# Query and key stages of a polysketch attention kernel: 32x32 TensorE tiles for the large units, and outer products with one factor in PSUM

## Chip, core and metric

The kernel runs on one core of a Trainium2 chip. The metric is the time on the device, in microseconds, of one execution. TensorE is called PE here, VectorE DVE, ScalarE ACT, GpSimd POOL and SyncE SP, as in the profile.

## What is computed

Four batches of four heads have q, k and v of 1088 positions by 32, and two sketches S1 and S2 of 8 x 32. The attention replaces the softmax by a product of two sketches; its result, with the heads side by side, goes through a two-layer network with the activation elu.

```python
def phi(x):
    a = np.einsum('rd,bhsd->bhsr', S1, x)
    b = np.einsum('rd,bhsd->bhsr', S2, x)
    return np.einsum('bhsi,bhsj->bhsij', a, b).reshape(*x.shape[:-1], r * r)
q_p, k_p = (phi(q), phi(k))
kv = np.einsum('bhsf,bhsd->bhfd', k_p, v)
z = np.sum(k_p, axis=2)
num = np.einsum('bhsf,bhfd->bhsd', q_p, kv)
den = np.einsum('bhsf,bhf->bhs', q_p, z)[..., None] + 1e-06
...
h = x @ w_in                              # 4352 x 128 by 128 x 2048
g = np.where(h > 0.0, h, alpha * (np.exp(np.minimum(h, 0.0)) - 1.0))
return (g @ w_out).astype(np.float32)     # 2048 x 128
```

Everything is float32. A feature vector is the outer product of two vectors of 8, so 64 numbers for each position and head.

## The kernel before, in words

**Steps.** The 68 half tiles of 64 positions (17 in each batch) are taken in nine groups g of eight, the last of four. d_ff is cut into eight pairs cp of 128 columns. A step is one (g, cp); the loop at L944 writes them out in a fixed order: groups 0 and 1 in turn, then groups 2 to 8, each with its eight cp. In step n PE computes `mm1` of step n (two PSUM tiles `h`, four buffers, L226), ACT and DVE make elu of it (`e`, two activations at L748 and L750; `gg`, L756), and PE then does the second matmul of step n-2. For groups 2 to 7 this second matmul is `mm2_seven` (L674): seven products of half size in place of eight, whose sums of the moving operand POOL makes (`tt`, L667 to L672). `W` holds the weights.

**The attention between the steps.** A table (`at`, `mid`, `late`, from L862) hangs single functions on a step: `at(n)` after mm1 of step n, `mid(n)` after the first half of elu, `late(n)` after the second half. Within an engine the order is the order of the calls; it is written out by hand and no scheduler changes it. Waits between engines follow from the tiles and their buffers.

- *Keys of batches 1 to 3* (L898): `transp` transposes k; `KF_late` (L315) projects it with 64x32 tiles of PE into two PSUM banks, `kfps`; `KF_late_out` transposes these to `abk` on DVE; `KO` (L334) forms the outer product `kp`, in two halves of 1280 and 1024 elements, on POOL for batch 1 and on DVE for batches 2 and 3; `KA` (L366) multiplies with v into the bank `kv`; `turn` and `turned` give `kvq` (L403, with a mask that keeps every second head) and the part of the denominator that is added to `SWq` (L395).
- *Queries of groups 2 to 8*, in units (L485): a unit is one group, or from group 4 on two groups. `un` counts its half tiles for each half of the partitions: 4 for units 2 and 3, 8 for units 4 and 6, 2 for unit 8. `queries` (L622) runs at steps 13, 15, 22, 30, 46 and 62, each time with q5 of one unit and q1 of the next: q5 with f = 0, then q1, then q5 with f = 1. `q1` (L502) multiplies the transposed q with `SWq`, `q1_out` transposes the result on DVE to `abw`; `q2_den` (L525) and `q2_half` (L580) form the quotient `an` and the outer product `qp` on DVE, `q4` transposes it to `qpT`; `q5` (L595) multiplies with `kvq`, and `q5_out` copies the result on ACT to `xg`, the input of mm1.

**Tiles of PE.** q1 and q5 use the array as four 64x64 tiles. A unit's positions are cut into two runs w, and the heads into two pairs r; in q1 the pair of heads is the row half and the run the column half, in q5 the other way round. A row half has a PSUM bank of its own. With 64 rows and two heads, the masked weights (`cmask`, the zeros of `SWq`) make half of the products zero. A matmul's length is the number of half tiles of its run that lie in one batch (`parts`, L492).

**PSUM.** Eight banks: four `h`, one each of `o0` and `o1`, and two with the tag `aux`, which the kfps, kv and query results share in turn. Where the results of q5 and q1 don't fit side by side in the two aux banks, `queries` takes the two `h` banks of the next step as well, before mm1 of that step writes them.

**Outer products.** `q2_half` and `KO` multiply a factor that is repeated along the inner axis by one that is repeated along the middle axis:

```python
nc.vector.tensor_mul(qp[g, i][:, :m], _ap(a_, list(a_.ap[1:]) + [[0, R]]),
                     _ap(b_, [b_.ap[1], [0, R], b_.ap[2]]))
```

Both factors lie in SBUF here.

Of the kernel before, what the change touches and what calls it, by code (L numbers as in the profile page):

```python
# [12 lines left out]
F32 = mybir.dt.float32  # L13
# [9 lines left out]
def _ap(ap: bass.AP, free):  # L23
    return dataclasses.replace(ap, ap=[list(ap.ap[0])] + [list(x) for x in free])
# [3 lines left out]
def kernel(  # L28
# [21 lines left out]
    nc = tc.nc  # L50
    B, H, S, D = q.shape
    R = S1.shape[0]
    P = 128
    FD = H * D
# [4 lines left out]
    KT = (NT + 1) // 2  # L59
# [4 lines left out]
    const = ctx.enter_context(tc.tile_pool(name="const", bufs=1))  # L64
    work = ctx.enter_context(tc.tile_pool(name="wk", bufs=2))
    psum = ctx.enter_context(tc.tile_pool(name="psum", bufs=2, space=bass.MemoryType.PSUM))
# [6 lines left out]
    qT = [const.tile([FD, NT, 64], F32, name=f"qT{b}") for b in range(2)] * 2  # L73
# [142 lines left out]
    cmask = const.tile([P, 2], F32, name="cmask")  # L216
# [12 lines left out]
    def keep_warm(n, cols=256):  # L229
        for i in range(n):  # L230
            nc.tensor.matmul(idle[:, :cols], some[:, :P], some[:, :cols], skip_group_check=True)  # L231
# [26 lines left out]
    Sab = const.tile([FD, H, 2 * R], F32, name="Sab")  # L258
    SW = const.tile([FD, H, 3, R], F32, name="SW")
    SWq = const.tile([FD, B, 2, 4, R], F32, name="SWq")  # L260
    keep_warm(3)
    keep_warm(1, 128)
    sps = psum.tile([P, 512], F32, name="sps", tag="aux")
# [24 lines left out]


    kvS = const.tile([P, H, D], F32, name="kvS")  # L290
    kvq = const.tile([P, B, 2, H, D], F32, name="kvq")
    kv_ps, kvz, feats, wzs, kf_ps = {}, {}, {}, {}, []


# [32 lines left out]
    def KF_late_out(b):  # L327
        ps = feats[b]
        ab = feats[b] = work.tile([P, 2, KT, H, R], F32, name="abk", tag="abk", bufs=2)
        for g2 in range(2):  # L330
            nc.vector.transpose(ab[:, :, :, 2 * g2:2 * g2 + 2, :].rearrange("p x t c r -> p t x (c r)"),
                                ps[g2][:, :32 * KT].rearrange("p (t x y) -> p t x y", x=2, y=2 * R))

    def KO(b, half, eng=nc.vector):  # L334
        kp = work.tile([P, 5, H, R, R], F32, name="kp", tag="kp", bufs=3)
# [59 lines left out]
    def Z_share(b):  # L395
        z = wzs.pop(b)
        nc.gpsimd.tensor_add(SWq[:, b, :, 2, :], z[:, :2], z[:, 2:])

    def KV(b, ps):
        for f in range(2):  # L400
            halves(ps[:, 128 + P * f:128 + P * f + P], kvz[b][:, f].rearrange("p c s -> p (c s)"), ident[:])

    def KV_out(b, ps):  # L403
        nc.vector.tensor_mul(kvq[:, b].rearrange("p f (g c) d -> p (f g) c d", c=2),
                             ps[:, 128:384].rearrange("p (x c d) -> p x c d", c=2, d=D),
                             _ap(cmask[:], [[0, 4], [1, 2], [0, D]]))


    def Z_first():
# [21 lines left out]
    NQ = (NH + 7) // 8  # L431
    qn = [min(8, NH - 8 * g) // 2 for g in range(NQ)]
    abw, ans, qp, qpT, xg, xps = {}, {}, {}, {}, {}, {}
# [4 lines left out]
    def half_tile(g, k):  # L438
        return divmod(8 * g + k, NT)
# [45 lines left out]
    units = {g: ([g, g + 1] if 4 <= g < NQ - 1 else [g]) for g in [2, 3] + list(range(4, NQ, 2))}  # L485
    un = {g: sum(qn[x] for x in gr) for g, gr in units.items()}
# [2 lines left out]

    def parts(g, w):  # L492

        n = un[g]
        k = 0
        while k < n:
            b, t = half_tile(g, n * w + k)
            m = min(n - k, NT - t)
            yield b, t, k, m
            k += m  # L500

    def q1(g, ps, start, o):  # L502
        todo = [(j, w, r, x) for w in range(2) for r in range(2) for j, x in enumerate(parts(g, w))]
        for j, w, r, (b, t, k, m) in sorted(todo, key=lambda x: x[0]):
            rows = slice(64 * r, 64 * r + 64)
            nc.tensor.matmul(ps[r][64 * w:64 * w + 64, o + 64 * k:o + 64 * (k + m)],  # L506
                             SWq[rows, b].rearrange("p c x r -> p (c x r)"),
                             qT[b][rows, t:t + m, :].rearrange("p t s -> p (t s)"), start=start and j == 0, stop=True,
                             skip_group_check=True, tile_position=(64 * r, 64 * w))
        abw[g] = ps, o  # L510

    def q1_out(g):
        (ps, o), n = abw[g], un[g]
        pair = n > 4
        abw[g] = work.tile([P, H * n if pair else H * 4, 4 * R], F32, name="abw", tag="abwp" if pair else "abw",
                           bufs=1 if pair else 2)
        for r in range(2):
            nc.vector.transpose(abw[g][:, 2 * n * r:2 * n * r + 2 * n, :].rearrange("p m y -> p (m y)"),
                                ps[r][:, o:o + 64 * n])

    def q2(g, parts=1):
        q2_den(g)
# [54 lines left out]
    def heads(g):  # L577
        return 2 if un[g] > 4 else H

    def q2_half(g, i):  # L580
        m = heads(g) * un[g]
        r = slice(m * i, m * i + m)
        qp[g, i] = work.tile([P, 4 * H, R, R], F32, name="qp", tag="qp", bufs=2)
        a_, b_ = ans[g][:, r], abw[g][:, r, :R]
        nc.vector.tensor_mul(qp[g, i][:, :m], _ap(a_, list(a_.ap[1:]) + [[0, R]]),
                             _ap(b_, [b_.ap[1], [0, R], b_.ap[2]]))

# [5 lines left out]
                            qp.pop((g, i))[:, :m].rearrange("p m i j -> p (m i j)"))  # L593

    def q5(g, ps, f):  # L595
        n = un[g]
        todo = [(j, w, r, x) for r in range(2) for w in range(2) for j, x in enumerate(parts(g, w))]
        for j, w, r, (b, t, k, m) in sorted(todo, key=lambda x: x[0]):
            i, o = (r, 0) if n > 4 else (0, 2 * n * r)
            rows = slice(64 * w, 64 * w + 64)  # L600
            nc.tensor.matmul(ps[w][64 * r:64 * r + 64, 64 * k:64 * (k + m)],  # L601
                             kvq[rows, b, f, 2 * r:2 * r + 2, :].rearrange("p c d -> p (c d)"),
                             qpT[g, i][rows, o + 2 * k:o + 2 * (k + m), f, :],
                             start=(f == 0 and j == 0), stop=(f == 1),
                             skip_group_check=True, tile_position=(64 * w, 64 * r))
        xps[g] = ps

    def q5_out(g, i=0):

        ps, n = xps[g], 64 * un[g]  # L610
        pair = len(units[g]) > 1
        x = xg[g + i] = work.tile([P, 512], F32, name="xg", tag="xg", bufs=3)
        for w in [i] if pair else range(2):
            if pair:
                to = x[:]
            elif g < NQ - 1:
                to = x[:, n * w:n * w + n]
            else:
                to = x[:, :2 * n].rearrange("p (k w s) -> p w k s", w=2, s=64)[:, w]
            nc.scalar.copy(to, ps[w][:, :n] if g < NQ - 1 else ps[w][:, :n].rearrange("p (k s) -> p k s", s=64))  # L620

    def queries(g5, g1, n):  # L622

        nx, nq = (64 * un[g] if g is not None else 0 for g in (g5, g1))
        if nx + nq > 512:
            hs[steps[n]] = [psum.tile([P, 512], F32, name="h", tag="h", bufs=4) for c in range(2)]
        aux = [psum.tile([P, 512], F32, name="qps", tag="aux") for _ in range(2)]
        if nx + nq > 512:
            xb, qb, o = [hs[steps[n]][0], aux[0]], [hs[steps[n]][1], aux[1]], 0
        else:  # L630
            xb, qb, o = aux, aux, nx

        if g5 is not None:
            q5(g5, xb, 0)
        if g1 is not None:
            q1(g1, qb, o == 0, o)
        if g5 is not None:
            q5(g5, xb, 1)


    hs, es, gs, ops = {}, {}, {}, {}
# [214 lines left out]
    steps = [(0, 0), (0, 1), (1, 0), (1, 1)] + [(g, cp) for cp in range(2, NP) for g in range(2)]  # L856
# [5 lines left out]
    def at(n, f, *a):  # L862
        extra.setdefault(n, []).append((f, *a))
# [4 lines left out]
    def late(n, f, *a):  # L868
        extra.setdefault((n, 1), []).append((f, *a))
# [22 lines left out]
    def turned(b):  # L892
        Z_out(b, kv_ps[b])
        KV_out(b, kv_ps[b])
        Z_share(b)


    for b, (n_t, n_f, n_o, n_a, n_z) in enumerate(  # L898
            ((4, 6, (7, 9), 11, 12), (15, 16, (17, 18), 19, 20), (17, 18, (23, 24), 27, 28)), 1):
        at(n_t, transp, kT, "k", b, 0, NT)  # L900
        at(n_f, KF_late, b)
        late(n_f, KF_late_out, b)
        for half in range(2):
            at(n_o[half], KO, b, half, nc.gpsimd if b == 1 else nc.vector)
        at(n_a, KA, b)
        late(n_a, sums_out, b)
        at(n_z, turn, b)
        late(n_z, turned, b)
# [16 lines left out]
    late(19, q2_half, 3, 0)  # L925
    late(20, q4, 3)
    late(22, q2_den, 4)
    at(26, q2_half, 4, 0)
    late(26, q2_half, 4, 1)
    late(27, q4, 4, 0)  # L930
    late(28, q4, 4, 1)
    late(31, q2_den, 6)
    late(32, q2_half, 6, 0)
    late(36, q2_half, 6, 1)
    late(37, q4, 6, 0)
    late(38, q4, 6, 1)
# [7 lines left out]
    for n in range(2, N + 2):  # L944
        if n < N:
            g, cp = steps[n]
# [26 lines left out]
        g, cp = steps[n - 2]  # L973
# [39 lines left out]
```

## Time and profile before

| | |
|---|---|
| timed runs | 269.57 us (268.58 to 269.76, three runs) |
| profiled execution, span | 267.13 us |
| PE, DVE, ACT, POOL busy | 98%, 71%, 68%, 62% |
| granted PE clock | 0.998 |
| DMA, mean | 51 GB/s, 49 GB/s of it HBM |

The profile is of one execution. An engine's busy time is the time in which it has an instruction in flight; matmuls overlap, so PE's share alone does not tell whether it is at its peak. Each float32 matmul of the code appears as two records, each with a weight load (PEld). "64*64 64x512" stands for a tile of 64 rows by 64 columns of the array and 512 moving columns. In a timeline a line gives start, length, engine, line of the kernel, operation, tiles and count; a bracket at its end gives the idle time of the engine before it and what ended that.

### The profile page before, as it was taken

The page shows a single profiled execution, that of the slowest core. Times are in us where ns is not written, and L with a number is a line of the kernel's source. Part 1 is how long each engine was busy: PE and PEld are TensorE (multiplying, and loading weights), DVE is VectorE, ACT ScalarE, POOL GpSimd, SP SyncE. Part 2 cuts the span into 40 slices and gives each one's busy share as a digit, 9 for nine tenths or more (in the row PEclk, how much of TensorE's full clock was granted, in tenths as well). Part 3 has the DMA queues.
Part 4 walks back from the last instruction along what each step waited for, and adds up shares of the span by engine and source line. Part 5 has one row for each costly group of instructions (what it writes and reads, how often), then busy time and mean ns, then how long its engine had stood idle before and what let it go on. Part 6 is the DMA issues. An engine that isn't in the chain of part 4 may idle for free.

```text
span 267.1 us, 7343 instructions
## 1 busy us (share of the span) xinstructions
PE 260.9 (98%) x2947; PEld 154.5 (58%) x2947; DVE 189.2 (71%) x342; ACT 181.5 (68%) x341; POOL 165.1 (62%) x230
## 2 busy tenths in 40 slices
PE   8899999999999999999999999999999999999994
PEld 6753333343333675658566666666766666666884
DVE  6799999996959896997649767554346444673652
ACT  2389978676566475766567777777677777777782
POOL 4400008204317986699969999998598888898300
PEclk9999999999999999999999999999999999999999
DMA  6996960011002200001100110001001100010011
GB/s 191 344 351 200 273 193 4 0 40 48 0 0 42 42 4 0 2 2 19 26 2 0 21 22 2 0 14 21 10 4 19 22 4 1 14 19 12 2 32 30
DMA packets 26418, 13.58 MB, mean 51 GB/s; under 512 B 19217, under 2 KB 24593, under 8 KB 26385
## 3 DMA queue, kind: packets, MB, share of 16 engines
q1 hardware_dynamic: 25792, 12.66, 18.2%
q8 instruction: 23, 0.38, 0.6%
q10 hardware_dynamic: 592, 0.46, 0.5%
q14 instruction: 11, 0.08, 0.1%
HBM read 10.88 MB, written 2.23 MB: 49 GB/s over the span
## 4 chain that ended last, share of the span: by engine, by line
PE 92%; DVE 4%; POOL 1%; ACT 1%; issue 1%; DVEq 0%
PE h L226 41%; PE pb L687 15%; PE pa L687 12%; PE o L226 11%; PE ol L226 3%; PE idle L231 2%; PE kv L371 1%; PE qps L601 1%; PE h L601 1%; DVE qp L549 1%; PE kfps L321 1%; PE h L506 1%; POOL tt L670 1%; PE kv L226 1%; PE abp L302 1%
## 5 line engine op out<-in xcount | busy, mean ns | idle before, releaser
L756 DVE SCALAR_TENSOR_TENSOR gg<-e,h 128x512 f32<-128x512 f32 (+1 forms) x144 | 92.4, 653 | 66.4 <-ACT e L750 65.1
L226 PE MATMUL h<-xg,W 128*64 128x512 f32 (+1 forms) x584 | 128.7, 563 | 0.0
L748 ACT ACTIVATE e<-h 128x512 f32<-128x512 f32 (+1 forms) x144 | 81.4, 565 | 56.1 <-PE h L226 52.9
L750 ACT ACTIVATE e<-e 128x512 f32<-128x512 f32 (+1 forms) x144 | 87.5, 607 | 4.4
L226 PEld LDWEIGHTS h<-xg,W 128*64 128x64 f32 x584 | 40.2, 137 | 47.3 <-issue 37.6
L670 POOL TENSOR_TENSOR tt<-gg 128x256 f32<-128x256 f32 x48 | 39.2, 817 | 12.1 <-DVE gg L756 11.6
L667 POOL TENSOR_TENSOR tt<-gg 128x256 f32<-128x256 f32 x48 | 35.1, 731 | 14.5 <-DVE gg L756 14.2
L672 POOL TENSOR_TENSOR tt<-gg,tt 128x256 f32<-128x256 f32 x48 | 38.4, 801 | 3.8
L671 POOL TENSOR_TENSOR tt<-tt,gg 128x256 f32<-128x256 f32 x48 | 36.0, 750 | 3.8
L687 PEld LDWEIGHTS pa<-gg,W 128*64 128x64 f32 x384 | 23.6, 137 | 23.7 <-issue 23.3
L226 PE MATMUL o<-gg,W 128*64 128x512 f32 x128 | 30.5, 597 | 0.4 <-DVE W L129 0.4
L687 PE MATMUL pa<-gg,W 128*64 128x128 f32 x384 | 29.5, 274 | 0.0
L687 PE MATMUL pb<-tt,SS 128*64 128x128 f32 x384 | 29.2, 273 | 0.0
L687 PEld LDWEIGHTS pb<-tt,SS 128*64 128x64 f32 x384 | 22.6, 137 | 0.0
L126 POOL TENSOR_TENSOR raw<-raw,tiny 128x512 f32<-128x512 f32 x1 | 1.0, 1045 | 29.8 <-DVE raw L121 29.8
L687 PE MATMUL pa<-tt,SS 128*64 128x128 f32 x192 | 18.7, 273 | 0.2 <-POOL tt L671 0.2
L687 PE MATMUL pb<-gg,SS 128*64 128x128 f32 x192 | 18.7, 273 | 0.0
L687 PE MATMUL pb<-tt,W 128*64 128x128 f32 x192 | 18.7, 273 | 0.0
L226 PEld LDWEIGHTS o<-gg,W 128*64 128x64 f32 x128 | 8.5, 136 | 16.2 <-issue 13.8
L687 PEld LDWEIGHTS pa<-tt,SS 128*64 128x64 f32 x192 | 12.1, 137 | 0.4 <-POOL tt L671 0.4
L687 PEld LDWEIGHTS pb<-gg,SS 128*64 128x64 f32 x192 | 12.1, 137 | 0.2 <-issue 0.2
L687 PEld LDWEIGHTS pb<-tt,W 128*64 128x64 f32 x192 | 12.2, 137 | 0.0
(139 smaller groups left out, 246.6 us busy)
## 6 DMA issues: line engine op xcount, KB each, us to landing
raw<-in_moe_w_in_dram SPq DMA_DIRECT2D x8, 256.0 KB, 5.5
raw<-in_moe_w_out_dram SPq DMA_DIRECT2D x8, 256.0 KB, 5.7
hd_k<-in_k_dram SPq DMA_DIRECT2D x3, 544.0 KB, 8.0
hd_q<-in_q_dram SPq DMA_DIRECT2D x3, 544.0 KB, 3.7
v<-in_v_dram SPq DMA_DIRECT2D x4, 288.0 KB, 6.8
out_dram<-ob SPq DMA_DIRECT2D x72, 16.0 KB, 1.5
v<-in_v_dram SPq DMA_DIRECT2D x4, 256.0 KB, 8.1
out_dram<-ob SPq DMA_DIRECT2D x16, 32.0 KB, 1.7
```

The source lines that it names most:

```text
L226: nc.tensor.matmul(dst[64 * u:64 * u + 64], lhs[:, 64 * u:64 * u + 64], rhs, skip_group_check=True, tile_position=(0, 64 * u), **kw)
L231: nc.tensor.matmul(idle[:, :cols], some[:, :P], some[:, :cols], skip_group_check=True)
L302: nc.tensor.matmul(ps[i // 5][64 * u:64 * u + 64, 64 * (i % 5):64 * (i % 5) + 64], kT[b][:, u * KT + i, :], Sab[:].rearrange("p h y -> p ( ...
L601: nc.tensor.matmul(ps[w][64 * r:64 * r + 64, 64 * k:64 * (k + m)], kvq[rows, b, f, 2 * r:2 * r + 2, :].rearrange("p c d -> p (c d)"), qpT[ ...
L667: nc.gpsimd.tensor_tensor(t[:, 0], b12, b11, op=SUB)
L670: nc.gpsimd.tensor_tensor(t[:, 2], b22, b12, op=SUB)
L671: nc.gpsimd.tensor_tensor(t[:, 1], t[:, 2], b11, op=ADD)
L672: nc.gpsimd.tensor_tensor(t[:, 3], b21, t[:, 1], op=SUB)
L687: nc.tensor.matmul(bank[64 * u:64 * u + 64, P * col:P * col + P], lhs, rhs[:, u], start=(first and i in (0, 3)), stop=last, skip_group_che ...
L748: nc.scalar.activation(e, hs[g, cp][c][:, :n], RELU, scale=-1.0)
L750: nc.scalar.activation(e, e, EXP, scale=-1.0)
L756: nc.vector.scalar_tensor_tensor(gs[g, cp][:, c, :n], es[g, cp][:, c, :n], -1.0, hs[g, cp][c][:, :n], op0=ADD, op1=MAX)
```

## The change

Units with `un` = 8 use sixteen 32x32 tiles, one head to a row or column quarter and four runs of positions, with the weights `SWs` (the sum of the two masked parts of `SWq`) and `kvs` (the unmasked kv). The other units keep 64x64. With four row quarters, q1 and q5 of these units write four banks (two `h` and two `aux`), 256 columns each. Where q5 and q1 of a call use different tiles, q5 with f = 0 and f = 1 now come one after the other, and q1 after both. `KO` of batches 2 and 3 and `q2_half` of units 4 and 6 read the factor `a` from an aux bank, to which ACT copies it a half step or more earlier. `KF_late` of batch 3 and its output move from step 18 to step 21, the first `q2_half` of unit 6 from step 32 to 33.

```diff
-    kvq = const.tile([P, B, 2, H, D], F32, name="kvq")
+    kvq = {b: const.tile([P, 2, H, D], F32, name=f"kvq{b}") for b in (0, 1, 3)}
+    kvs = {b: const.tile([P, 2, H, D], F32, name=f"kvs{b}") for b in (1, 2, 3)}
...
+    def KO_a(b, half):
...
+        p = feats[b, half, "a"] = psum.tile([P, 512], F32, name="ka", tag="aux")
+        nc.scalar.copy(p[:, :n], feats[b][:, 1, t].rearrange("p t h r -> p (t h r)"))
+    def KO_b(b, half):
...
+        nc.vector.tensor_mul(kp[:, :t.stop - t.start].rearrange("p t h i j -> p (t h) i j"),
+                             _ap(a_, list(a_.ap[1:]) + [[0, R]]), _ap(b_, [b_.ap[1], [0, R], b_.ap[2]]))
...
     def Z_share(b):
         z = wzs.pop(b)
         nc.gpsimd.tensor_add(SWq[:, b, :, 2, :], z[:, :2], z[:, 2:])
+        if b:
+            nc.gpsimd.tensor_add(SWs[:, b - 1], SWq[:, b, 0], SWq[:, b, 1])
...
     def KV_out(b, ps):
+        if b in kvs:
+            copy = nc.scalar.copy if b in kvq else nc.vector.tensor_copy
+            copy(kvs[b][:].rearrange("p f h d -> p (f h d)"), ps[:, 128:384])
+        if b in kvq:
...
+    def wide_tiles(g):
+        return un[g] < 8
     def parts(g, w):
-        n = un[g]
+        n = un[g] if wide_tiles(g) else un[g] // 2
...
+    def q1(g, ps, o, opened):
+        s = 64 if wide_tiles(g) else 32
+        n = P // s
+        todo = [(j, w, r, x) for w in range(n) for r in range(n) for j, x in enumerate(parts(g, w))]
...
+            nc.tensor.matmul(ps[r][s * w:s * w + s, o + 64 * k:o + 64 * (k + m)], lhs,
+                             qT[b][rows, t:t + m, :].rearrange("p t s -> p (t s)"),
+                             start=j == 0 and not any(ps[r] is x for x in opened), stop=True,
+                             skip_group_check=True, tile_position=(s * r, s * w))
...
     def q1_out(g):
-        for r in range(2):
+        m = H * n // len(ps)
+        for r in range(len(ps)):
...
+    def q2_a(g, i):
+        m = heads(g) * un[g]
+        p = psum.tile([P, 512], F32, name="qa", tag="aux")
+        ans[g, i] = p[:, :m * R].rearrange("p (m r) -> p m r", r=R)
+        nc.scalar.copy(p[:, :m * R], ans[g][:, m * i:m * i + m].rearrange("p m r -> p (m r)"))
...
     def queries(g5, g1, n):
+        banks = lambda g: 0 if g is None else 2 if wide_tiles(g) else 4
+        if banks(g5) + banks(g1) > 4:
             hs[steps[n]] = [psum.tile([P, 512], F32, name="h", tag="h", bufs=4) for c in range(2)]
         aux = [psum.tile([P, 512], F32, name="qps", tag="aux") for _ in range(2)]
+        ps = {2: aux, 4: hs.get(steps[n], []) + aux}
+        same = banks(g5) == banks(g1)
         if g5 is not None:
-            q5(g5, xb, 0)
+            q5(g5, ps[banks(g5)], 0)
+            if not same:
+                q5(g5, ps[banks(g5)], 1)
         if g1 is not None:
-            q1(g1, qb, o == 0, o)
-        if g5 is not None:
-            q5(g5, xb, 1)
+            q1(g1, ps[banks(g1)], 256 if g5 is not None else 0, ps[banks(g5)] if g5 is not None else [])
+        if g5 is not None and same:
+            q5(g5, ps[banks(g5)], 1)
...
-            ((4, 6, (7, 9), 11, 12), (15, 16, (17, 18), 19, 20), (17, 18, (23, 24), 27, 28)), 1):
+            ((4, 6, (7, 9), 11, 12), (15, 16, (17, 18), 19, 20), (17, 21, (23, 24), 27, 28)), 1):
...
-            at(n_o[half], KO, b, half, nc.gpsimd if b == 1 else nc.vector)
+            if b == 1:
+                at(n_o[half], KO, b, half, nc.gpsimd)
+            else:
+                late(n_o[half] - 1, KO_a, b, half)
+                at(n_o[half], KO_b, b, half)
...
+    for n, g, i in ((25, 4, 0), (26, 4, 1), (32, 6, 0), (35, 6, 1)):
+        late(n, q2_a, g, i)
...
-    late(32, q2_half, 6, 0)
+    late(33, q2_half, 6, 0)
```

q5 changes as q1 does, and `q5_out` copies two banks of 256 columns to each `xg` in place of one of 512.

## Prediction

> **What bounds the kernel now.** I read the page first, its busy shares and its chain of waits, then the timeline of single engines. A step is one pass of the loop at L944; I number steps by counting the groups of `h` matmuls.
>
> ```profile
> PE 260.9 (98%) x2947; PEld 154.5 (58%) x2947; DVE 189.2 (71%) x342; ACT 181.5 (68%) x341; POOL 165.1 (62%) x230
> ...
> PE 92%; DVE 4%; POOL 1%; ACT 1%; issue 1%; DVEq 0%
> PE h L226 41%; PE pb L687 15%; PE pa L687 12%; PE o L226 11%; PE ol L226 3%; PE idle L231 2%; PE kv L371 1%; PE qps L601 1%; PE h L601 1%; DVE qp L549 1%; PE kfps L321 1%; PE h L506 1%; POOL tt L670 1%; PE kv L226 1%; PE abp L302 1%
> ```
>
> TensorE is busy 98% and carries 92% of the chain. A busy PE need not be at its peak, so the starts in its timeline decide. Around step 30 (columns: start, length, engine, line, operation):
>
> ```profile
> 130.27 1.89 PE L226 MATMUL h<-xg,W 128*64 128x512 f32 x8
> 132.09 0.32 PE L601 MATMUL h<-qpT,kvq 64*64 64x128 f32 x1
> 132.09 0.64 PE L601 MATMUL qps<-qpT,kvq 64*64 64x512 f32 x1
> ...
> 133.01 0.59 PE L506 MATMUL h<-qT,SWq 64*64 64x512 f32 x1
> ...
> 133.87 0.59 PE L601 MATMUL qps<-qpT,kvq 64*64 64x512 f32 x1
> ...
> 134.83 0.66 PE L687 MATMUL pa<-gg,W 128*64 128x128 f32 x8
> ...
> 136.41 1.89 PE L226 MATMUL h<-xg,W 128*64 128x512 f32 x8
> 138.12 0.61 PE L687 MATMUL pa<-gg,W 128*64 128x128 f32 x8
> ...
> 139.65 1.89 PE L226 MATMUL h<-xg,W 128*64 128x512 f32 x8
> ```
>
> From 136.41 to 139.65 an ordinary step takes 3.24 us: 1.71 for eight `h` records, the rest for 28 records of L687. A pair of 512-column records on two column tiles takes 1.71/4 = 0.43 us, a pair of 128-column records 0.11: PE is bound by its columns, with no gap. So a column less on PE is time off the end, as long as nobody else makes PE wait.
>
> The query group of step 30 runs from 132.09 to 134.83. It has three phases, q5 f=0, q1 and q5 f=1, starting at 132.09, 133.00 and 133.87: 0.86 to 0.91 each, two 512-column records on each of four 64x64 tiles. It starts 0.10 after 130.27 + 1.72, and about 0.05 is lost in the first round after each change of tile size.
>
> Only one later stretch has PE waiting for another engine, steps 25 to 27:
>
> ```profile
> 111.07 1.37 DVE L286 TENSOR_TENSOR kp<-abk 128x1024 f32<-128x1024 f32 x1
> 111.32 1.72 POOL L670 TENSOR_TENSOR tt<-gg 128x256 f32<-128x256 f32 x1
> 113.11 0.73 POOL L671 TENSOR_TENSOR tt<-tt,gg 128x256 f32<-128x256 f32 x1
> ...
> 113.90 0.44 PE L687 MATMUL pa<-tt,SS 128*64 128x128 f32 x4 [0.16 <-POOL tt L671]
> ```
>
> POOL's L670, 0.73 elsewhere, takes 1.72 while DVE forms an outer product; `tt` is late, and PE with it. The L687 group at 113.13 lasts 1.91, the one at 116.76 lasts 1.71, where an undisturbed one lasts 1.53: 0.38 + 0.18, and 0.03 at 118.46, 0.59 us in all. DVE has no idle time from 105.92 to 123.
>
> **What the Trainium skill says.** "TensorE: Matmul & The Clock Gate", section "Measured speedup vs the span model": sixteen 32x32 tiles of 512 columns ran 10.6 times as fast as one after another, with about 4 ns between tiles. No run here has 32-row tiles; eight 64x32 tiles (`kfps`, 16 records of 288 columns) take 0.65 us from 85.64 to 86.29, where column time alone is 0.48, so eight do run side by side here. "TensorEngine Tiling (Array Packing)", "Key Properties": a change of tile size drains the array; the trace has 0.10 + 0.05 for it. "SBUF — State Buffer", "Who interferes with whom": a DVE operation with two SBUF inputs shuts out a GpSimd operation that reads SBUF, one with a single SBUF input does not; the 1.72 above agrees. "PSUM — Partial Sum Buffer", "PSUM bank collisions raise a hardware error": different row tiles may not write one bank at a time; the trace has one bank for each of the two row halves, and the change takes four for four.
>
> **The change part by part.** Sums are against the profiled span, 267.13 us; the three timed runs have a median of 269.57, and I carry the difference over.
>
> *32x32 tiles.* Only the two units with un = 8 change: 4 (q1 at step 22, q5 at 30) and 6 (q1 at 30, q5 at 46). Each tile streams 256 columns in place of 512, so a phase falls from 0.854 (4 x 0.427 / 2) to 0.427. Step 22: one phase, -0.43. Step 30: three, -1.28. Step 46: two, -0.85. Sum -2.56. Against it: steps 22 and 46 now mix both sizes, one change more each, 2 x 0.15 = +0.30. The tiles start one after another, some 7 ns apart (132.09 to 132.11 for four), so sixteen end about 0.08 later than four, in three groups: +0.25. The 40 records of a phase need 40 x 7 = 0.28 us to issue, under 0.427. **Net -2.0.** No 32-row tile is in the trace: if records cost 15 ns, as in the `kv` group (90 in 1.34), a phase takes 0.60 and six phases give back 1.0; if neither the extra change nor the stagger shows, -2.56. I take -2.0.
>
> *PSUM factor.* Eight outer products (KO for b = 2, 3, `q2_half` for units 4, 6) read one factor from PSUM. DVE: a 1024-element one takes 1.23 from PSUM (L354), the same as an undisturbed one from SBUF (69.41), but 1.34 to 1.70 while POOL works; 1280 elements 1.69 and 2.02, and about 1.23 + 256 x 1.04 ns = 1.49 from PSUM (the slope of L354: 256 elements 0.43, 1024 elements 1.23). In steps 23 to 27 DVE saves 0.53 + 0.14 + 2 x 0.12 = 0.9 and POOL three locks of about 0.95 (111.32, 118.30, and 120.91 at 1.60). PE's 0.59 goes: **-0.59**, with 0 as the other end. ACT gets eight copies: by L384 (32 elements, 0.17) and L620 (256, 0.38), about 0.9 ns an element, 0.26 to 0.29 each. ACT has 0.83 to 1.03 us idle before its first activation in nearly every step there; that hides them.
>
> *Waits added.* KO_a(b,0) stands in ACT's queue behind the two activations of its step and waits for DVE's KF_late_out (b = 2) or for q1_out to free the bank (b = 3); the next step's activations queue behind it. Then DVE waits for ACT before KO_b, with `gg` behind it, and PE wants `gg` two steps later. At 79.6 ACT has 1.83 us idle; at 105 it waited 0.72 anyhow. I take 0.
>
> *KF_late(3) from step 18 to 21.* Its PE time, 0.65 + 0.15, only moves: PE is 0.8 ahead from 18 to 21 and no more after. It passes KA(2), the turn of b = 2 and the groups of mm2. Its two DVE transposes (0.84) move from 88.84 to 100.77, where DVE has 1.30 us idle before 102.07. New is that q5(3) at step 22 needs the banks that they free: done near 101.0 to 101.6, against PE at 101.46. I take 0, at most 0.2.
>
> *q5 of one unit before q1 of the next (steps 22, 46).* ACT's two `xg` copies start at about 102.6 and not 103.47, so `gg` of step 22, 105.31 now, comes about 0.6 earlier, at the head of DVE's full stretch. q1_out takes four transposes of 0.39 for two of 0.70, +0.17 on DVE for each unit; q5_out four copies of 0.38 for two of 0.58, +0.35 on ACT: both beside PE, which is in L687 for 1.58 us after the group. At step 30 the two `h` banks are read first, some 0.9 us after PE leaves the group, before PE reaches the next `h`.
>
> *Small ones.* Three POOL adds of 0.22 (`SWs`): the first two stand in POOL's idle time (15.6 and 0.82), the third after `SWq` at 131.47, with q1(6) reading it 1.1 us or more later. `kvs`: two ACT copies of 0.37 with over 1.5 us idle before the next activation; b = 2 exchanges a DVE operation of 0.41 for a copy. All 0. No DMA is added, and SP's and POOL's queues keep their order.
>
> Sum: -2.0 - 0.59 = -2.6. Span 264.5, time 269.57 - 2.6 = **267.0 us**. About 0.5% (1.35 us) is what a measurement of this kernel tells from no change.
>
> **Rivals.**
> (a) *DVE keeps the stretch.* The locks go but the copies and the moved transposes keep DVE late; PE arrives earlier and waits the more, so that 0.6 to 1.4 of the 2.6 is lost: 267.6 to 268.4. For: no DVE idle from 105.92 to 123. Against: the 0.9 and 0.6 counted above.
> (b) *The tiles don't pay.* If only eight of sixteen stream at once, a phase stays at 0.854: +0.55 for changes and stagger, -0.59: 269.5, no change. For: no 32-row tile in the trace. Against: the 10.6 of the skill, `kfps`.
> (c) *Slower: the handshake.* Place: KO_b(3,0), KO_b(3,1), q2_half(4,0), q2_half(4,1) on DVE, steps 23 to 26. If each finds its ACT copy behind an activation pair (0.58 + 0.63 = 1.21), DVE loses 4 x 1.21 = 4.8, less the 1.2 that it gains net there, and PE, which now waits 0.59 and comes 0.3 earlier, waits 0.9 + 4.8 - 1.2 = 4.5 in all. -2.0 + (4.5 - 0.59) = +1.9: 271.5. It decides from some 4.3 us of DVE waiting. For: ACT and DVE now wait for each other in turn. Against: each copy is queued a step or half a step ahead, with ACT idle after it.
>
> **How the numbers follow.** Forecast 0.68 (266.0 to 267.6, the spread of -2.0 to -2.56 and of the runs); (a) 0.14, two thirds of it below 268.2; (b) 0.10; (c) 0.08. Faster 0.68 + 0.10 = 0.78; same 0.04 + 0.10 = 0.14; slower 0.08. The range 265.9 to 268.9 holds the forecast, (a) and the 15-ns records (268.0), and leaves (b) and (c) out.
>
> **What would show it.** Right: a query group of about 1.5 us at step 30; no L670 or L672 above 1.0 beside an outer product of b = 3 or of unit 4; L687 groups of 1.53 or 1.58 at steps 25 to 27; outer products of 1.23 and 1.49. Wrong: 32x32 records further apart than 15 ns; `ka` or `qa` copies that DVE waits for; PE waiting on an aux bank at step 22 or at KA(3) (step 27), whose bank q2_half(4,0) must free.

## The result and the profile after

| | before | after |
|---|---|---|
| timed runs, median | 269.16 us (268.58 to 269.76) | 267.84 us (267.27 to 268.26) |
| ratio, with 95% interval | | 0.9949 (0.9928 to 0.9971) |
| span of the profiled execution | 267.13 us | 266.5 us |
| first `kfps` matmul (step 4) to last matmul | 225.33 us | 224.24 us |
| query groups of steps 22, 30, 46 | 1.88, 2.74, 2.10 us | 1.82, 2.40, 1.97 us |
| `mm2_seven` groups of steps 25, 26 | 1.91, 1.71 us | 1.53, 1.53 us |

The change is faster by 1.3 us where 2.6 were forecast. The two spans differ by less still, because the start, up to the first `kfps` matmul, was 0.4 us longer in the profiled execution after; the fourth row leaves it out, and I use it for all kernels below: **1.09 us less**. A group's length is the time from its first matmul to the first of the next group. Line numbers of the kernel after: L542 is `q1`, L648 `q5`, L730 `mm2_seven`, L710 to L715 the sums `tt` on POOL, L350 `KO_b`, L628 `q2_half`.

The page of the kernel after, busy shares and chain:

```profile
PE 260.4 (98%) x3115; PEld 154.9 (58%) x3115; DVE 187.7 (70%) x346; ACT 183.9 (69%) x355; POOL 159.6 (60%) x233
...
PE 93%; DVE 4%; POOL 1%; issue 1%; ACT 0%; DVEq 0%
PE h L226 43%; PE pb L730 16%; PE pa L730 12%; PE o L226 11%; PE ol L226 3%; PE idle L231 2%; PE kv L391 1%; PE h L648 1%; PE qps L648 1%; DVE qp L586 1%; POOL kp L287 1%; PE kfps L323 1%; PE qps L542 1%; PE kv L226 1%; PE abp L304 1%
```

PE is the bound as before. It has 168 records more; POOL is busy 5.5 us less and `POOL tt` has left the chain. Step 30, PE's timeline (start, length, engine, line, operation, tiles, count of records):

```profile
131.89 0.41 PE L648 MATMUL h<-qpT,kvs 32*32 32x128 f32 x2
131.90 0.41 PE L648 MATMUL qps<-qpT,kvs 32*32 32x256 f32 x2
...
132.32 0.54 PE L648 MATMUL h<-qpT,kvs 32*32 32x128 f32 x5
132.58 0.36 PE L542 MATMUL h<-qT,SWs 32*32 32x192 f32 x2
...
133.29 0.40 PE L648 MATMUL h<-qpT,kvs 32*32 32x256 f32 x2
...
133.93 0.42 PE L648 MATMUL h<-qpT,kvs 32*32 32x128 f32 x5
134.29 0.66 PE L730 MATMUL pa<-gg,W 128*64 128x128 f32 x8
```

From 131.89 to 134.29 the three phases take 0.69, 0.59 and 1.12 (q5 f = 1 from 133.17), where 0.43 each was forecast. A phase is counted from its first matmul to the first of the next. The rows of 128 columns and five records are where the runs that a batch boundary cuts get their second matmuls.

The stretch where PE waited for POOL has gone. POOL's and PE's timelines at steps 25 and 26, with DVE's outer product at 110.96:

```profile
110.96 1.21 DVE L350 TENSOR_TENSOR kp<-ka,abk 128x1024 f32<-128x1024 f32 x1
```

```profile
111.21 0.73 POOL L713 TENSOR_TENSOR tt<-gg 128x256 f32<-128x256 f32 x1
112.02 0.73 POOL L714 TENSOR_TENSOR tt<-tt,gg 128x256 f32<-128x256 f32 x1
```

```profile
113.52 0.61 PE L730 MATMUL pa<-gg,W 128*64 128x128 f32 x8
113.95 0.39 PE L730 MATMUL pa<-tt,SS 128*64 128x128 f32 x4
```

The first `tt` beside the outer product takes 0.73, where it took 1.72, and no idle time stands behind the second matmul row of PE. Over the whole trace nine `tt` took more than 1 us before and two after; one of the two (1.60 at 93.91) lies beside the outer product of unit 3, which still reads both factors from SBUF.

So the sum has one good half and one bad: the waits gave back 0.59 as forecast, the tiles 0.53 in place of 2.0. The experiments ask first whether the halves stand alone, and then what the tiles pay.

### The profile page after: what moved, and what is told of

The parts are those of the page before. It is cut to its first block, busy times and chain, and to the rows that moved or that the text cites. A ratio compares the mean times of both kernels' runs of the same rounds, so it can differ in the third digit from the quotient of the medians.

```text
span 266.5 us, 7686 instructions
## 1 busy us (share of the span) xinstructions
PE 260.4 (98%) x3115; PEld 154.9 (58%) x3115; DVE 187.7 (70%) x346; ACT 183.9 (69%) x355; POOL 159.6 (60%) x233
## 4 chain that ended last, share of the span: by engine, by line
PE 93%; DVE 4%; POOL 1%; issue 1%; ACT 0%; DVEq 0%
PE h L226 43%; PE pb L730 16%; PE pa L730 12%; PE o L226 11%; PE ol L226 3%; PE idle L231 2%; PE kv L391 1%; PE h L648 1%; PE qps L648 1%; DVE qp L586 1%; POOL kp L287 1%; PE kfps L323 1%; PE qps L542 1%; PE kv L226 1%; PE abp L304 1%
## 5 line engine op out<-in xcount | busy, mean ns | idle before, releaser
L710 POOL TENSOR_TENSOR tt<-gg 128x256 f32<-128x256 f32 x48 | 35.1, 730 | 16.4 <-DVE gg L799 16.0
L713 POOL TENSOR_TENSOR tt<-gg 128x256 f32<-128x256 f32 x48 | 35.3, 736 | 14.4 <-DVE gg L799 14.0
L715 POOL TENSOR_TENSOR tt<-gg,tt 128x256 f32<-128x256 f32 x48 | 36.5, 760 | 3.8
L714 POOL TENSOR_TENSOR tt<-tt,gg 128x256 f32<-128x256 f32 x48 | 35.2, 733 | 3.8
L730 PEld LDWEIGHTS pa<-gg,W 128*64 128x64 f32 x384 | 23.6, 137 | 22.7 <-issue 22.0
L730 PE MATMUL pa<-gg,W 128*64 128x128 f32 x384 | 29.5, 275 | 0.0
L730 PE MATMUL pb<-tt,SS 128*64 128x128 f32 x384 | 29.1, 273 | 0.0
L730 PEld LDWEIGHTS pb<-tt,SS 128*64 128x64 f32 x384 | 22.6, 137 | 0.0
L730 PE MATMUL pb<-gg,SS 128*64 128x128 f32 x192 | 18.7, 273 | 0.0
L730 PE MATMUL pa<-tt,SS 128*64 128x128 f32 x192 | 18.6, 273 | 0.0
L730 PE MATMUL pb<-tt,W 128*64 128x128 f32 x192 | 18.6, 273 | 0.0
L730 PEld LDWEIGHTS pb<-tt,W 128*64 128x64 f32 x192 | 12.1, 137 | 0.0
L730 PEld LDWEIGHTS pa<-tt,SS 128*64 128x64 f32 x192 | 12.1, 137 | 0.0
L730 PEld LDWEIGHTS pb<-gg,SS 128*64 128x64 f32 x192 | 12.1, 137 | 0.1
```

What stands on the lines that cost most here:

```text
L710: nc.gpsimd.tensor_tensor(t[:, 0], b12, b11, op=SUB)
L713: nc.gpsimd.tensor_tensor(t[:, 2], b22, b12, op=SUB)
L714: nc.gpsimd.tensor_tensor(t[:, 1], t[:, 2], b11, op=ADD)
L715: nc.gpsimd.tensor_tensor(t[:, 3], b21, t[:, 1], op=SUB)
L730: nc.tensor.matmul(bank[64 * u:64 * u + 64, P * col:P * col + P], lhs, rhs[:, u], start=(first and i in (0, 3)), stop=last, skip_group_che ...
```

## The experiments

Each edit is against the kernel after, unless said otherwise.

### The two halves apart

e1 is the kernel before with the PSUM factor, its waits and its moved steps; e2 is the kernel after without them.

```diff
# e1, against the kernel before: 64x64 tiles everywhere, and
+ KO_a, KO_b, q2_a, ans.pop(...) in q2_half, as in the change
- (17, 18, (23, 24), 27, 28)
+ (17, 21, (23, 24), 27, 28)
# e2
- (17, 21, (23, 24), 27, 28)
+ (17, 18, (23, 24), 27, 28)
+ at(n_o[half], KO, b, half, nc.gpsimd if b == 1 else nc.vector)
-     late(n, q2_a, g, i)
```

> The kernel before with the factor in PSUM and its moved steps alone; q1 and q5 keep 64x64 tiles, two banks and their old order. Lock theory (DVE with two SBUF inputs shuts POOL out): no L670-type addition above 1.0 us beside an outer product of b = 3 or of unit 4, the 0.59 us of PE waiting at steps 25 to 27 gone, query groups unchanged at 1.88, 2.74 and 2.10 us; time 0.5 to 0.7 us under the kernel before. Rival (the waiting went because q5 now comes before q1 and gg of step 22 is earlier): at least 0.3 us of PE waiting stays.

> The changed kernel with the outer products and their steps as before (both factors in SBUF); 32x32 tiles kept. Lock theory: PE waits at steps 25 to 27 by 0.5 to 0.9 us as before. The three query groups stay at 1.82, 2.40 and 1.97 us, 0.53 us less than before in all; time 0 to 0.6 us under the kernel before. Rival: no waiting, and the time of the changed kernel, 1.3 us under.

Measured: e1 268.69 us, ratio 0.9979 (0.9963 to 0.9995), from the first `kfps` 224.78, which is 0.56 less than before; no `mm2_seven` group is longer than 1.58, the waits show none of PE from 80 us on, and the query groups are those of before to 0.001. e2 268.53 us, ratio 0.9983 (0.9966 to 1.0), 224.85, 0.48 less; groups 1.82, 2.40, 1.97, and the waits for `tt` are back (the POOL operation at 113.96 takes 1.71). 0.56 + 0.48 = 1.04 against 1.09 for both: the halves add up and don't lean on each other. In time each half is at the edge of what can be told from no change; the groups tell them apart.

### Is it the bank, or the order of the steps?

```diff
-        p = feats[b, half, "a"] = psum.tile([P, 512], F32, name="ka", tag="aux")
+        p = feats[b, half, "a"] = work.tile([P, 160], F32, name="ka", tag="ka")
-        p = psum.tile([P, 512], F32, name="qa", tag="aux")
+        p = work.tile([P, 160], F32, name="qa", tag="ka")
```

> The changed kernel with the copied factor in an SBUF tile in place of a PSUM bank; the copies, waits and steps are the same. Lock theory: outer products of 1.3 to 2.0 us, POOL additions of 1.6 to 1.9 beside them, and PE waiting at steps 25 to 27 of 0.3 to 0.9 us; time 0.3 to 0.9 us over the changed kernel. Rival (the order of the steps did it): same as the changed kernel, no PE waiting.

Copies, waits between engines and steps are those of the kernel after; only the place of the copied factor differs. Measured: 268.88 us, ratio 0.9991 (0.9976 to 1.0006), 225.09: 0.84 more than after. DVE's and POOL's timelines in the same stretch:

```profile
110.86 1.37 DVE L350 TENSOR_TENSOR kp<-ka,abk 128x1024 f32<-128x1024 f32 x1
```

```profile
111.11 1.71 POOL L713 TENSOR_TENSOR tt<-gg 128x256 f32<-128x256 f32 x1
112.90 0.73 POOL L714 TENSOR_TENSOR tt<-tt,gg 128x256 f32<-128x256 f32 x1
```

And PE's:

```profile
113.69 0.44 PE L730 MATMUL pa<-tt,SS 128*64 128x128 f32 x4 [0.21 <-POOL tt L714]
```

The 1.71, the longer outer product and PE's wait return together; three `mm2_seven` groups of 1.77, 1.96 and 1.70 are 0.24 + 0.43 + 0.17 = 0.84 longer than in the kernel after, the whole difference. With both factors in SBUF the DVE operation shuts POOL out, with one in PSUM it doesn't, as the Trainium skill has it ("SBUF — State Buffer", "Who interferes with whom"). The order of the steps explains none of the gain. The first of the three groups, at 85.10, is not long in the kernel before or in e2: there `KF_late` of batch 3 stands before it, while in e3 PE comes to it about 0.75 us sooner and POOL's sums do not. Without the bank the copies and the moved steps are thus a small loss (225.09 against 224.85 in e2), and the bank's 0.84 pays for that as well.

### Does each record cost its start?

```diff
-            m = min(n - k, NT - t)
+            m = min(n - k, NT - t, n if wide_tiles(g) else 2)
```

> The changed kernel with each matmul of the 32x32 units cut to at most 128 columns: 200 records in place of 120 at step 30, 152 for 88 at step 46, 80 for 56 at step 22, over the same columns. Issue theory (a weight load and a matmul cost PE about 16.7 ns whatever their columns): the groups grow by 80, 64 and 24 records x 16.7 ns, 1.3, 1.1 and 0.4 us, to 3.7, 3.0 and 2.2. Column theory (32-row tiles stream more slowly, or share a bus): the groups stay within 0.2 us of 2.40, 1.97 and 1.82.

At most 128 columns to a matmul, so 24, 80 and 64 records more at steps 22, 30 and 46, with the same columns. (A float32 matmul is two records.) Measured: 271.85 us, ratio 1.009 (1.006 to 1.012); groups 2.02, 4.28, 2.39. Step 30 has a hole:

```profile
134.27 0.33 PE L648 MATMUL h<-qpT,kvs 32*32 32x128 f32 x2
135.98 0.30 PE L648 MATMUL qps<-qpT,kvs 32*32 32x128 f32 x2 [1.38 <-issue]
```

PE waits 1.65 us there from start to start for nothing that the profile shows; without it the group is 2.63. A second such wait lengthens the `mm2_seven` group at 190.87 by 0.56. What is left are 0.20, 0.23 and 0.42 for 24, 80 and 64 records, 3 to 8 ns for each, so a cost of 16.7 ns for every *record* is out. The column theory fails too, at step 46, where it allowed 0.2. A cost for every *matmul* of two records is not excluded: 12 more at step 22 with 16.7 ns each would be the 0.20 measured, 32 more at step 46 0.53 for the 0.42 measured. Step 30 decides nothing here: after the hole the matmuls start 6 to 11 ns apart and not 16.7, so the hole also saved time.

### Is it the cut runs?

17 half tiles in a batch don't divide by four, so in units 4 and 6 one of the four runs is cut, and each phase has 20 matmuls on 16 tiles: four tiles get a second one while the first may still stream. In e5 no run is cut:

```diff
             m = min(n - k, NT - t)
+            if not wide_tiles(g):
+                t = min(t, NT - n)
```

> The changed kernel, but no 32-row unit ever cuts a run of half tiles at a batch boundary: every one of the sixteen tiles gets one matmul a phase and none a second one (16 matmuls in place of 20 in a phase). Left out: the positions beyond a batch boundary in units 4 and 6 are computed from other positions of the same batch. Theory 1, the second matmul on a tile that is still busy holds up all matmuls behind it: the query groups fall from 1.82 / 2.40 / 1.97 us (steps 22, 30, 46) to about 1.80 / 1.70 / 1.64, and the time by about 1.0 us, to a ratio of about 0.991 against the kernel before. Theory 2, the matmuls merely start 16.7 ns apart and each costs that: four fewer in a phase save 0.07 us each, groups 1.75 / 2.20 / 1.84, ratio about 0.9935. Theory 3, the sixteen tiles do not stream side by side at all: groups unchanged to 0.05.

Measured: 267.02 us, ratio 0.9925 (0.9906 to 0.9944), 223.61; groups 1.68, 2.06, 1.80. That is 0.14 + 0.34 + 0.17 = 0.65 less than after, for 4 + 12 + 8 = 24 second matmuls: **27 ns each**, although the columns are the same. Neither theory had the size: the first promised 1.05 at these steps, the second 0.40, the third nothing. So the cut runs cost more than their starts, but they are not the larger part of what is missing. That part can be seen in PE's timeline of e5 (L650 is q5, L544 q1):

```profile
131.07 0.41 PE L650 MATMUL h<-qpT,kvs 32*32 32x256 f32 x2
131.08 0.41 PE L650 MATMUL qps<-qpT,kvs 32*32 32x256 f32 x2
...
131.16 0.41 PE L650 MATMUL qps<-qpT,kvs 32*32 32x256 f32 x2
131.31 0.38 PE L650 MATMUL h<-qpT,kvs 32*32 32x256 f32 x2
...
131.52 0.59 PE L544 MATMUL h<-qT,SWs 32*32 32x256 f32 x2
131.73 0.40 PE L544 MATMUL qps<-qT,SWs 32*32 32x256 f32 x1
...
131.90 0.41 PE L544 MATMUL h<-qT,SWs 32*32 32x256 f32 x2
131.93 0.41 PE L544 MATMUL qps<-qT,SWs 32*32 32x256 f32 x2
...
132.36 0.41 PE L650 MATMUL qps<-qpT,kvs 32*32 32x256 f32 x2
...
132.80 0.39 PE L650 MATMUL qps<-qpT,kvs 32*32 32x256 f32 x2
133.12 0.55 PE L732 MATMUL pa<-gg,W 128*64 128x128 f32 x6
```

Nearly every row here is a pair of tiles. In the first phase, queued while PE was still in `h`, the pairs start 13 ns apart, 6.7 ns a matmul; all sixteen tiles have started within 0.10 us, and the second record of the first tile comes only at 131.31, so sixteen tiles do work side by side. The next phase sends one matmul at 131.52, 0.21 after that record, when its tile is free, and the second only 0.19 later, at 131.72 (the first row of L544 holds both); from 131.73 on a pair starts every 33 ns, **16.7 ns a matmul**. f = 1 sends two as their tiles come free and the third again 0.19 after the second, at 132.36. So the phases don't run into each other as the tiles come free.

Counted from these points (131.07, 131.72, 132.36, 133.12), the three phases of step 30 take 0.65, 0.65 and 0.76; the two of step 46 take 0.65 and 0.78. The averages, 0.69 and 0.71, are near 15 x 16.7 ns + 0.43 of columns, 0.68, but the trace shows two different costs behind them: a phase that is followed by another loses to the hole of 0.19, and the last one of a group to its slow starts. Why there is a hole is not settled by any run here. PE's weight loads have it too: one starts at 131.53, the next at 131.71.

### Can the second matmuls be put elsewhere?

e6 takes the tiles of the cut run first and spreads the four second matmuls over the last six others of the phase; e8 keeps them back and puts one after every third matmul of the next 32-row phase; e9 takes q5's tiles by row group, the cut one first, with the second matmuls last. e7 leaves them alone and moves a phase.

```diff
# e6: order of a phase
+ out = first + rest[:6], then rest[6:] and the second parts in turn
# e8: order of a phase
+ after every third matmul one second part of the phase before
# e9: q5 with 32 rows (q1 has this order already)
-        todo = [... for r in range(n) for w in range(n) ...]
+        todo = [... for w in range(n) for r in range(n) ...]
# e7: step 30 as f = 0, f = 1, q1
-        same = banks(g5) == banks(g1)
+        same = banks(g5) == banks(g1) == 2
```

> The changed kernel, with another order inside a 32-row phase: first the four first parts of the row group whose runs are cut, then the other matmuls, and the four second parts put between the last six of those. Theory 1 (a second matmul on a busy tile holds up what is behind it): the first parts of that row group started some 0.1 us before the phase's tail instead of just before their second parts, so less is held up; step 30 falls from 2.40 to about 2.0 to 2.2, step 46 from 1.97 to about 1.8. Theory 2 (each matmul costs its start): no change, 2.40 and 1.97, since the number of matmuls is the same.

> The changed kernel, but at step 30 both halves of q5 run before q1, in place of q5 f=0, q1, q5 f=1. Theory 1 (second matmuls on busy tiles): the phase after another one on the same tiles pays wherever it stands; step 30 stays at 2.3 to 2.4 us (1.59 for the two halves, as at step 46, and 0.7 to 0.8 for q1). A rival, that the last phase is long (1.03 against 0.69) because it comes back to banks that q1 has used in between: step 30 falls to about 2.0.

> The changed kernel, with the second parts of a 32-row phase kept back and put one by one, after every third matmul, into the 32-row phase that follows, and at the end of the group or before a 64-row phase where none follows. Theory 1 (a second matmul on a busy tile holds up what is behind it): kept back long enough they hold up nothing; step 30 falls from 2.40 to about 1.9, step 46 from 1.97 to about 1.75, step 22 (one phase) stays at 1.8; ratio against the kernel before about 0.992 to 0.9935. Theory 2 (each matmul costs its start, whatever stands before it): unchanged, 2.40 and 1.97, ratio 0.995.

> The changed kernel, with the tiles of a 32-row q5 phase taken in another order: the row group whose runs are cut first, so that its four second matmuls, still last in the phase, come to tiles that have been started longest ago. Theory A (a second matmul waits for its own tile, and so does what stands behind it): they wait less, step 30 falls from 2.40 to 2.25, step 46 from 1.97 to 1.87, step 22 stays at 1.82. Theory B (the first matmul on a tile that is already in use lets the next one start only about one of its own passes later, however long its tile has been started; q1 at step 22 already has this order and pays 0.138 for its four): no gain, 2.35 to 2.5 and 1.95 to 2.05.

| | groups of steps 22, 30, 46, us | first `kfps` to the end | time, ratio (95%) |
|---|---|---|---|
| after | 1.82, 2.40, 1.97 | 224.24 | 0.9949 (0.9928 to 0.9971) |
| e6 | 2.04, 2.47, 2.19 | 224.75 | 268.42, 0.9978 (0.9969 to 0.9988) |
| e7 | 1.82, 2.33, 1.97 | 224.16 | 267.28 (one run) |
| e8 | 1.82, 2.53, 2.11 | 224.49 | 268.29, 0.9967 (0.9958 to 0.9976) |
| e9 | 1.82, 2.16, 1.84 | 223.85 | 267.59, 0.9945 (0.9926 to 0.9963) |

e6 and e8 missed: both are slower than the kernel after, by 0.51 and 0.25, where they should have been faster. Theory 2, no change, is out with that; the kind of effect was right and my choice of places wrong. In e6 at step 22 the matmuls ahead of the second ones start within 0.10 us, and the last full-length ones, which stand behind second ones, only 0.45 us after the first of the phase; in e8, by the order of the calls, the tiles have by then got the next phase's matmul. e9 gives each cut tile the longest time: groups fall by 0.24 and 0.13, more than theory A said (0.15 and 0.10), and theory B, which said no gain, is out. For sixteen second matmuls of q5 that is 24 ns each, nearly all that e5 found for one. e9 also changes the order of the uncut tiles, and no run parts the two. e7's 0.07 lies near "stays", and its rival (banks that q1 has used in between) is out.

### The fastest order, beside the kernel after

e10 is e7 again, timed; e11 has both orders; e12 is the kernel after.

> The kernel with q5 f=0 and f=1 before q1 at step 30 once more, now timed, as the fastest one with a whole output so far. From its group at step 30 (2.33 in place of 2.40) 0.07 us less than the changed kernel: ratio 0.9945 against the kernel before, which no measurement here can tell from 0.9949.

> Both orders together: the cut row group first in q5's 32-row phases, and at step 30 q5 f=0, f=1, then q1. Theory A (a second matmul waits for its own tile): the two gains are at different places, 0.24 + 0.13 from the first at steps 30 and 46, 0.07 from the second; step 30 about 2.09, step 46 1.84, and 0.44 us less than the changed kernel, ratio about 0.993 against the kernel before. If the second order gained by taking the late second matmuls of one phase out of the way of another, the first has taken that already: step 30 stays at 2.15, ratio 0.9935.

> The changed kernel itself once more, on the same chip as the fastest version, so that the two can be set side by side: groups 1.82, 2.40 and 1.97, ratio 0.995 against the kernel before.

Measured: e10 267.55 us, 0.9945 (0.9928 to 0.9962), step 30 2.34. e11 267.88 us, 0.9949 (0.9934 to 0.9963), groups 1.82, 2.15, 1.83, 223.86. e12 268.05 us, 0.9963 (0.9943 to 0.9983), groups 1.82, 2.40, 1.98, 224.23. At step 30 e11 stays at e9's 2.15: the order of the phases gained only what the order of the tiles takes anyway. PE's work is 0.37 us shorter in e11 than in e12, the medians of 22 runs each differ by 0.17, and the runs of each spread over 2 us or more: the trace shows the gain, the time does not establish it. e9 is the simpler edit; by the traces it and e11 take 0.4 us off the kernel after.

## Why the prediction was right, and where not

**Right: what bounds it, and the sign.** PE is bound by its columns, and PE time taken out comes off the end: in every kernel the sum over groups and waits gives the total (after: 0.53 + 0.59 = 1.12 against 1.09; e6 against after: 0.21 + 0.07 + 0.22 = 0.50 more, against 0.51).

**Right: the PSUM factor, -0.59.** The L730 groups at steps 25 and 26 are 1.53, as undisturbed ones were before; L350 takes 1.21 for 1024 elements and 1.45 to 1.48 for 1280 (forecast 1.23 and 1.49), L628 1.20. e1 alone gives 0.56, and e3, with only the bank exchanged, takes 0.84 back.

**Right: waits, copies and moves at nothing, with the bank.** The copies take 0.26 to 0.30, and in the waits of the trace nobody waits for them; one stands 1.5 us in ACT's queue until `abk` is there, and PE loses nothing by it. PE waits for no aux bank at step 22 or 27. Rivals (a) and (c) leave no mark: in e1, where the handshake stands alone, PE does not wait there.

**Wrong: "Net -2.0" for the tiles; it was -0.53.** The columns were counted rightly, and two terms of the sum were mis-sized.

- *The stagger, +0.25.* I took 7 ns from one start to the next, which holds for matmuls that were queued ahead (6.7 measured), and charged it once for each group, as if later phases followed on the tiles as they come free. They don't, and later matmuls start 16.7 ns apart. By group, without cut runs (e5 against before): step 22, with one 32-row phase, -0.20, just what the forecast's own terms give (-0.43 + 0.15 + 0.08); step 30, three phases, -0.68 for -1.20; step 46, two phases, -0.29 for -0.62. The miss is 0.52 + 0.33 = 0.85 for three phases that follow another, some 0.28 each. The trace of e5 has it in two parts: each of the three phases that another follows takes 0.65 and not 0.43, 0.19 of the 0.22 being the hole before the next phase; and the last phase of steps 30 and 46 takes 0.76 and 0.78, where the single one of step 22, most of it queued ahead, takes 0.66. 3 x 0.22 + 0.10 + 0.12 = 0.88.
- *The records, +0.* "40 x 7 = 0.28 us to issue, under 0.427" hid eight of the forty records: second matmuls on tiles in use. They cost 0.65 (e5), up to 0.38 of which was only their order (e9).

-2.0 + 0.85 + 0.65 = -0.5, as measured. The prediction's own signs of being wrong are there: the group of step 30 takes 2.40 and not about 1.5, and 32x32 matmuls in a series start 16.7 ns apart, where more than 15 was the sign. Rival (b), that the tiles don't pay at all, came nearer for this term (+0.55), but not in its reason: sixteen tiles do stream side by side. The bound with a phase of 0.60 (268.0) lies nearest to the time, though by another rate: 15 ns a record, where a matmul of two records takes 16.7. I took the 7 ns between four starts of the trace before over it; four starts that were queued ahead say nothing of a long series.

That 267.84 us still lies in the range of 265.9 to 268.9 is in part luck. The sum missed half of the 2.6. The range held because it left room for rival (a) and for the 15-ns records; and 0.4 us of the nearness to 267.0 comes from the kernel before, which took 269.16 in six runs and not the 269.57 that I started from. One reading was also off, without weight in the sum: of the three phases of step 30 before, "0.86 to 0.91 each", the third takes 0.96, from 133.87 to 134.83.

The Trainium skill ("TensorE: Matmul & The Clock Gate", "Measured speedup vs the span model") has about 4 ns between tiles, for a single set of sixteen. Here it is 6.7 for matmuls that were queued ahead and 16.7 for those that follow; the measurement decides, and the model doesn't carry over to sets one after another.

## What to carry to other kernels

Before splitting a matmul over more and smaller tiles, look for the start distance of a *long* series, and charge a loss to each set, not once for all. Here columns plus 15 times 16.7 ns, 0.68 us, came near the average of the sets (0.69 and 0.71); that this sum holds for other shapes is not shown. Keep every tile to one matmul in a set; where one must have two, start that tile first and put its second matmul last, which gave 0.4 us here by the trace. And where DVE and POOL work at the same time, the place of an operand (PSUM or SBUF) can be worth more than the operation: moving one factor, with a copy on an engine that has time, took 0.59 us of waiting off an engine that neither of them is.

## What the runs showed that I had not expected

- Start distances of 32x32 matmuls in float32: 6.7 ns for those queued ahead, 16.7 ns after; and at a change of phase one or two matmuls go ahead while the next comes only 0.19 us later.
- A place in the order decides the sign: second matmuls spread out cost 0.51 us more than after, the same ones behind tiles that started first 0.40 us less.
- Two waits of PE for nothing that the profile shows, 1.65 and 0.56 us, in e4, whose query groups have 24 to 80 records more; from 80 us on no other kernel's waits show one of this kind. What PE lacked there was not tried.
